# Re-ordering the issue lists of a fused SSM-convolution and token-MLP kernel, with the last spectrum pair's transfers on SyncE and GpSimd

## The chip, the cores and the metric

The kernel runs on one core of a Trainium2 chip. The metric is the device time of one execution in microseconds (us), taken as the median over runs. Besides the runs there is one profiled execution, from which every duration below is read. Times on the profile's axis count from the start of its span.

## The reference, cut to what matters

```python
def _A_ref(q, k, v, shift_k, ssm_k, ssm_D):        # S = 2048 tokens, D = 448 channels
    ...
    kv = k_shift * v                               # k filtered over 4 tokens, times v
    kv_f = rfft2(pad(kv, S)); kf_f = rfft2(pad(ssm_k, S))
    y = irfft2(kv_f * kf_f)[:S]                    # causal convolution of length 2048
    y = y + kv * ssm_D
    return q * y

def _B_ref(x, w1, b1, w2, b2):                     # F = 1792
    h = layernorm(x)
    u = gelu(einsum("bsd,sf->bdf", h, w1) + b1)    # the MLP mixes tokens, not channels
    y = einsum("bdf,fs->bds", u, w2) + b2
    return transpose(y)

x = A_q
h = x + _A_ref(layernorm(x), A_k, A_v, A_shift_k, A_ssm_k, A_ssm_D)
out = h + _B_ref(layernorm(h), B_w1, B_b1, B_w2, B_b2)
```

## The kernel before, in words

A token index is split in two: 128 partitions times 16 rows r. The convolution is done as a two-step Fourier transform on TensorE. Stage 1 (steps k1 and u1, L1060) transforms over one factor; its output is moved between partitions by SBUF-to-SBUF DMAs (L1076); stage 2 (k2 and u2, L1095) transforms over the other. Then the spectra of the filter and of kv are multiplied and transformed back. The way back is where the change lies.

**Inverse stage 1 (emit_products_i1).** It works on eight pairs jj of frequency groups. For each pair VectorE multiplies the two spectra (two products, L1161), TensorE does 16 matmuls (L1178), and ScalarE copies the two PSUM halves, h = 0 and 1, into the buffer TU (L739 in the profile, which is the helper that records every such copy). DMAs then carry the result from TU to the buffer TZ, where the partitions are those that the next stage contracts over. For seven of the pairs each of the two groups of a pair takes two DMAs (L1201): one of 196 KB for rows 0 to 13, by GpSimd (for one group of pair 1 by SyncE), and one of 28 KB for rows 14 and 15, by SyncE. The last pair, number 7, is cut differently, by halves h and groups par: four DMAs of 98 KB (L1190).

**Rows 0 and 1 in advance (emit_ct, NZ = 2).** The places of the last pair in TZ are filled with zeros for rows 0 and 1 (L1119), and what the last pair gives to these rows is added by extra matmuls (L1308) that read TU directly and use a small table EW. EW is filled by four DMAs of 4 KB from the table ET (L1128); these are the small table transfers.

**Inverse stage 2 (emit_i2).** For each row r two matmuls (L1300) contract TZ with the table ET. VectorE, ScalarE and GpSimd then apply the gate with the normalised input, take a layer norm (two rows at a time from row 2 on, with the powers on GpSimd at L1379) and write the normalised row Q (L1386 on VectorE). The PSUM copy is on VectorE for rows 0 to 3 (L1337), and else on ScalarE (L1317) or VectorE (L1319), as the order says; L1327 is VectorE's gate product and L1355 ScalarE's sum of squares.

**MLP (emit_mlp).** As soon as Q of row r is there, seven matmuls (L1433) add row r to the first seven chunks of the hidden layer; they hold seven of the eight PSUM banks, so that the rows of stage 2 that still come share one bank, each waiting for the copy of the one before it. Then come the other seven chunks (L1443), the GELUs, the second layer (L1455), the residual add (L1458) and the output DMAs. The weights of the first layer come in quarters w1a.0 to w1a.3 (L1406) and w1b (L1410), those of the second in w2 (L1417), all on SyncE's queue. w1a.1 waits for all four DMAs of the last pair.

**The order.** Every engine's instruction list is written out by hand, in the table ORDER at the top of the file, and each engine runs its list strictly in order; a scheduler only puts in the semaphore waits and picks the PSUM banks. A token such as i1.16:19 is step i1.16, operation 19. These tokens are used below:

| Token | What it is |
|---|---|
| i1.1, i1.4, i1.6, i1.8, i1.10, i1.12, i1.14, i1.16 | inverse stage 1 of pairs 0 to 7, in this order; on PE and ACT matmuls and copies, from 18 or 19 on the DMAs |
| i1.4:20 | the 196 KB DMA of pair 1 that SyncE issues; i1.4:18 is GpSimd's |
| i1.16:19, :20, :21, :22 | the last pair's DMAs: (h 0, par 0), (h 0, par 1), (h 1, par 0), (h 1, par 1) |
| i1.16:18, i1.16:9 | ScalarE's copies of the last pair's halves h 1 and h 0 |
| ct0.1:2 to :5 | the four small table transfers into EW (L1128) |
| i2.1, i2.9, i2.17, i2.20, i2.28, i2.32, i2.41, i2.45, i2.54, ... i2.84, i2.93, i2.97 | stage 2 matmuls of rows 0, 1, 2, 3, 4, 5, 6, 7, 8, ... 13, 14, 15; i2.2 and i2.10 are the extra matmuls of rows 0 and 1 |
| i2.3, i2.4, i2.5, i2.6, i2.7, i2.8 | row 0 behind its matmuls: gate, statistics on DVE, power on POOL (i2.7), Q on DVE (i2.8) |
| mlp.0 ... mlp.15 | the L1433 matmuls of row r, seven each |
| q.4 ... q.8, xn.* | statistics of the input rows (DVE L1237, L1239; powers POOL L1245, L1248) and the normalised input rows 0 to 3 (ACT L1270) |
| warm.* | 14 matmuls whose result is never read (L1211), put where TensorE would wait |

SyncE's list from the last pairs on, before:

```
i1.6:22 ct0.1:5 ct0.1:2-4 i1.4:20 i1.16:22 i1.16:20 i1.16:19 i1.1:20 i1.1:22 w1a.1:0
i1.12:22 i1.14:20 i1.4:21 i1.4:19 w1a.2:0 i1.6:20 i1.14:22 i1.10:20 i1.10:22 w1a.3:0
i1.8:22 i1.12:20 i1.8:20 w1b.0:0-3 w2.0:0-3
```

Of the kernel before, what the change touches and what calls it, by code (L numbers as in the profile page):

```python
# [36 lines left out]
        "mlp.15:1 mlp.15:5-6 mlp.15:3 mlp.15:2 mlp.17:0-15 mlp.18:0-15 mlp.19:0-15 mlp.20:0-15 mlp.21:0-15 "
        "mlp.22:0-15 mlp.23:0-15 mlp.24:0-13 mlp.25:0-13 mlp.26:0-13 mlp.27:0-13 mlp.28:0-13 mlp.29:0-13 "
# [545 lines left out]
def _build(nc, A_q, A_k, A_v, A_shift_k, A_ssm_k, A_ssm_D, B_w1, B_b1, B_w2, B_b2, out):  # L584
# [54 lines left out]
    with ctx:  # L639
        sch = _Sched(nc, ctx, n_dma_sems=112, small_off=SMALL)  # L640
        op = sch.op
# [509 lines left out]
        def emit_products_i1():  # L1151
            for jj in range(R // 2):
# [44 lines left out]
                for par in range(2):  # L1197
                    j = 2 * jj + par
# [319 lines left out]
```

## Time and profile before

| | |
|---|---|
| median of 3 runs | 173.64 us (172.6, 173.64, 174.01) |
| the profiled execution's own time | 173.4 us |
| its span | 171.6 us, so 1.8 us lie around the span |
| granted TensorE clock | 0.999 |
| busy over the span | PE 162.0 us, VectorE 101.4, ScalarE 92.6, GpSimd 59.5 |
| inverse stage 1, last pair's matmuls | 69.62 to about 71.3 us |
| stage 2 with the first MLP rows | 74.87 to 94.66 us |
| rest of the MLP | to about 169 us |

The page of the profile gives busy time by engine and the costliest groups. The view of the chain of waits goes back from the last instruction and says, in order of time, which engine or transfer held the end. The timeline gives start and duration of the instructions of one engine, merged where they follow each other, and in brackets the idle time before them and what ended it. Two things are needed to read TensorE here: a 448-column matmul has a duration of 0.35 us, but the next one starts 0.19 us later, so a wait costs what its start is late against the 0.19 us pitch, which is about 0.16 us more than the idle time in the bracket. And a wait for several semaphores is put down to the one that came last by the profile, which need not be the one that was waited for.

### The profile page before, as it was taken

The page shows a single profiled execution, that of the slowest core. Times are in us where ns is not written, and L with a number is a line of the kernel's source. Part 1 is how long each engine was busy: PE and PEld are TensorE (multiplying, and loading weights), DVE is VectorE, ACT ScalarE, POOL GpSimd, SP SyncE. Part 2 cuts the span into 40 slices and gives each one's busy share as a digit, 9 for nine tenths or more (in the row PEclk, how much of TensorE's full clock was granted, in tenths as well). Part 3 has the DMA queues.
Part 4 walks back from the last instruction along what each step waited for, and adds up shares of the span by engine and source line. Part 5 has one row for each costly group of instructions (what it writes and reads, how often), then busy time and mean ns, then how long its engine had stood idle before and what let it go on. Part 6 is the DMA issues. An engine that isn't in the chain of part 4 may idle for free.

```text
span 171.6 us, 3572 instructions
## 1 busy us (share of the span) xinstructions
PE 162.0 (94%) x1425; PEld 94.4 (55%) x1425; DVE 101.4 (59%) x188; ACT 92.6 (54%) x132; POOL 59.5 (35%) x151
## 2 busy tenths in 40 slices
PE   6979999889889999988999999999999999999994
PEld 2765745442334344543454555555567777777783
DVE  7998988859899999999979730000003133132231
ACT  3798688988999999989857526321210000000000
POOL 8347527590810586246887830000000000000000
PEclk9999999999999999999999999999999999999999
DMA  5999677685859756546999999991000111101111
GB/s 164 419 310 381 200 240 281 223 315 174 268 140 370 279 168 195 176 161 179 285 316 372 408 423 415 418 419 60 0 0 4 53 53 53 53 0 57 53 53 54
DMA packets 15652, 35.15 MB, mean 205 GB/s; under 512 B 3692, under 2 KB 9804, under 8 KB 15636
## 3 DMA queue, kind: packets, MB, share of 16 engines
q1 hardware_dynamic: 12588, 28.45, 46.0%
q0 software_dynamic: 2784, 6.29, 11.6%
q8 instruction: 11, 0.18, 0.4%
q10 hardware_dynamic: 264, 0.18, 0.3%
q14 instruction: 5, 0.04, 0.1%
HBM read 22.05 MB, written 1.84 MB: 139 GB/s over the span
## 4 chain that ended last, share of the span: by engine, by line
PE 64%; ACT 15%; DMA 9%; DVE 5%; SPq 2%; POOL 2%; issue 2%; DVEq 0%; POOLq 0%
PE ps L1455 25%; PE ps L1443 12%; PE ps L1433 9%; ACT arena L739 8%; PE ps L1095 5%; DMA arena<-in_A_ssm_k_dram 5%; ACT arena L1070 4%; DMA arena<-arena 4%; PE ps L1178 4%; PE ps L1060 3%; PE ps L993 2%; PE ps L1300 2%; DVE arena L1008 2%; ACT arena L740 2%; SPq L888 1%
## 5 line engine op out<-in xcount | busy, mean ns | idle before, releaser
L1458 DVE SCALAR_TENSOR_TENSOR arena<-ps,arena 128x448 bf16<-128x448 f32 (+2 forms) x17 | 11.1, 656 | 57.2 <-PE ps L1455 57.2
L1455 PE MATMUL ps<-arena 128*128 128x448 bf16 (+2 forms) x238 | 42.7, 342 | 0.0
L1455 PEld LDWEIGHTS ps<-arena 128*128 128x128 bf16 x238 | 33.3, 145 | 9.5
L739 ACT CAST arena<-ps 128x896 bf16<-128x896 f32 x30 | 24.6, 1013 | 0.2 <-PE ps L1095 0.2
L1433 PE MATMUL ps<-arena 128*128 128x448 bf16 x112 | 22.6, 353 | 0.2 <-DVE arena L1375 0.2
L1070 ACT CAST arena<-ps 128x896 bf16<-128x896 f32 x24 | 20.5, 915 | 3.8 <-PE ps L1060 3.7
L1076 POOL DMA_DIRECT2D arena<-arena x32 | 17.6, 556 | 13.1 <-ACT arena L1070 11.4
L1443 PE MATMUL ps<-arena 128*128 128x448 bf16 x112 | 21.4, 352 | 0.0
L1423 ACT ACTIVATE arena<-ps,arena 128x448 bf16<-128x448 f32 x14 | 8.3, 635 | 19.1 <-PE ps L1443 14.6
L1095 PE MATMUL ps<-arena 128*64 128x448 bf16 x128 | 15.2, 359 | 2.4 <-ACT arena L739 0.8
L1161 DVE TENSOR_TENSOR arena<-arena 128x1792 bf16<-128x1792 bf16 x16 | 16.7, 1085 | 0.3 <-ACT arena L739 0.2
L1433 PEld LDWEIGHTS ps<-arena 128*128 128x128 bf16 x112 | 10.8, 98 | 10.9 <-DVE arena L1386 1.2
L1443 PEld LDWEIGHTS ps<-arena 128*128 128x128 bf16 x112 | 11.0, 98 | 10.2
L1060 PE MATMUL ps<-arena 128*32 128x448 bf16 x256 | 15.0, 355 | 0.8 <-DVE arena L1008 0.5
L1178 PE MATMUL ps<-arena 64*128 64x448 bf16 x128 | 14.5, 351 | 0.1
L1201 POOL DMA_DIRECT2D arena<-arena x13 | 7.7, 599 | 13.7 <-ACT arena L739 13.7
L1095 PEld LDWEIGHTS ps<-arena 128*64 128x64 f16 x128 | 5.8, 108 | 10.8 <-ACT arena L739 2.9
L1178 PEld LDWEIGHTS ps<-arena 64*128 64x128 f16 x128 | 6.1, 94 | 8.2 <-ACT arena L739 2.5
L1008 DVE TENSOR_TENSOR arena<-ps,arena 128x512 bf16<-128x512 f32 (+1 forms) x16 | 9.1, 618 | 2.1 <-PE ps L993 1.8
L1355 ACT ACTIVATE arena<-arena 128x448 bf16<-128x448 f32 x14 | 8.0, 572 | 3.6 <-DVE arena L1327 3.5
L739 ACT COPY arena<-ps 128x1024 bf16<-128x1024 bf16 (+1 forms) x8 | 7.8, 1016 | 3.7 <-PE ps L967 2.9
L1386 DVE TENSOR_SCALAR arena<-arena 128x448 bf16<-128x448 f32 x16 | 7.7, 505 | 2.8 <-POOL arena L1379 2.8
(96 smaller groups left out, 192.1 us busy)
## 6 DMA issues: line engine op xcount, KB each, us to landing
arena<-in_B_w_dram SPq DMA_DIRECT2D x8, 896.0 KB, 7.2
arena<-in_B_w_dram SPq DMA_DIRECT2D x2, 2048.0 KB, 17.8
arena<-arena POOLq DMA_DIRECT2D x32, 112.0 KB, 3.3
arena<-arena SPq DMA_DIRECT2D x16, 224.0 KB, 3.1
arena<-in_B_w_dram SPq DMA_DIRECT2D x2, 1536.0 KB, 20.1
arena<-arena POOLq DMA_DIRECT2D x13, 196.0 KB, 4.2
arena<-in_A_k_dram SPq DMA_DIRECT2D x4, 448.0 KB, 5.8
arena<-in_A_v_dram SPq DMA_DIRECT2D x4, 448.0 KB, 9.1
```

Of the source, the lines that this page charges most:

```text
L739: return e.copy(out=dst(), in_=src())
L1008: return e.tensor_tensor(out=v, in0=u.rearrange("p t (r d) -> p t r d", d=64), in1=v, op=ALU.mult)
L1060: op("pe", lambda e, W, b=b, r=r, q=q, x=x, c0=c0: e.matmul(PS[32 * q:32 * q + 32, b.slots[x], 0:D], E[:, 2 * r + x, c0:c0 + 32], src[:, r ...
L1070: return e.copy(out=dst, in_=Ppair(b)) if W == "act" else e.tensor_copy(out=dst, in_=Ppair(b))
L1076: shuf[tag].append(op(q_, lambda e, W, g=g, i=i, a=a, nu=nu, jh=jh: e.dma_start(T[a + i:a + i + 4 * nu - 3:4].rearrange("p (j k) c d -> p ...
L1095: op("pe", lambda e, W, b=bs[h], h=h, j=j, c=c, par=par: e.matmul(PS[64 * par:64 * par + 64, b.slots[c], 0:D], FW[:, 64 * c:64 * c + 64], ...
L1161: op("dve", lambda e, W, m=m, i=i: e.tensor_tensor(out=MR(m.slots[0]).rearrange("p (x y) d -> p x y d", x=2), in0=TU[:, i].unsqueeze(2).br ...
L1178: k = op("pe", lambda e, W, b=bs[h], m=ms[h], par=par, t=t, tab=tab, xy=xy, P=P: e.matmul(Pb(b, par), tab[P, :], MR(m.slots[0])[P, xy, :], ...
L1433: op("pe", lambda e, W, r=r, fc=fc, b=bs[fc]: e.matmul(Pb(b), W1A[:, r, 128 * fc:128 * fc + 128], Q[:, r, :], start=(r == 0), stop=(r == R ...
L1443: op("pe", lambda e, W, r=r, fc=fc, b=b: e.matmul(Pb(b), W1B[:, r, 128 * (fc - n0):128 * (fc - n0) + 128], Q[:, r, :], start=(r == 0), sto ...
L1455: op("pe", lambda e, W, r=r, fc=fc, b=b, d0=d0, d1=d1: e.matmul(Pb(b)[:, d0:d1], W2[fc // 7][:, fc % 7, r:S:R], G[:, fc, d0:d1], start=(fc ...
L1458: op("dve", lambda e, W, r=r, b=b, A=A, d0=d0, d1=d1: e.scalar_tensor_tensor(out=X[:, r, d0:d1], in0=Pb(b)[:, d0:d1], scalar=bm[:, r:r + 1 ...
```

## The change

One line of code and the order lists. In emit_products_i1 the last pair's DMAs go to SyncE where h equals par (i1.16:19 and :22) and to GpSimd where it does not (:20 and :21); before, ScalarE issued :21 and SyncE the other three. In SyncE's list the small table transfers stand behind i1.10:20 instead of i1.6:22, and all 28 KB DMAs stand ahead of w1a.3. On TensorE, from the last pair on, the table transposes come first, the warm matmuls are spread (nine instead of eight behind the last pair's matmuls), and rows 2, 7, 3, 4, 6, 8, 5 are taken in this order instead of 4, 2, 7, 3, 6, 5, 8; row 11 comes behind mlp.3 instead of mlp.2, row 12 behind mlp.4 instead of mlp.3. On ScalarE and VectorE the order of the same operations changes, and rows 12 and 13 swap engines for their PSUM copy (i2.81 to VectorE, i2.85 to ScalarE). Up to the last pair's matmuls the lists of TensorE, ScalarE, VectorE and GpSimd are unchanged but for one warm matmul.

```diff
     "pe": (
...
-        "i1.4:16 warm.9:0 warm.11:0 warm.5:0 warm.8:0 warm.1:0 i1.16:1-7 i1.16:10-16 i1.16:8 i1.16:17 warm.10:0 "
-        "warm.4:0 warm.7:0 warm.6:0 warm.0:0 ct.2:0-7 warm.12:0 warm.3:0 ct.0:0-7 ct.1:0-6 warm.2:0 i2.1:0-1 "
-        "i2.2:0-3 i2.9:0 ct.1:7 i2.9:1 i2.10:0-3 i2.28:0-1 i2.17:0-1 i2.45:0-1 i2.20:0-1 i2.41:0-1 i2.32:0-1 "
-        "i2.54:0-1 mlp.0:6 mlp.0:1 mlp.0:5 mlp.0:2-4 mlp.0:0 i2.58:0-1 mlp.1:6 mlp.1:0 mlp.1:4 mlp.1:3 mlp.1:2 "
...
+        "i1.4:16 warm.9:0 warm.11:0 warm.5:0 warm.8:0 i1.16:1-7 i1.16:10-17 i1.16:8 ct.1:0-7 ct.0:0-7 ct.2:0-7 "
+        "warm.1:0 warm.10:0 warm.6:0 warm.3:0 i2.1:0-1 i2.2:0-3 i2.9:0-1 i2.10:0-3 warm.0:0 warm.2:0 i2.17:0-1 "
+        "i2.45:0-1 i2.20:0-1 warm.4:0 warm.7:0 i2.28:0-1 i2.41:0-1 warm.12:0 i2.54:0-1 i2.32:0-1 mlp.0:4 mlp.0:1 "
+        "mlp.0:5 mlp.0:3 mlp.0:6 i2.58:0-1 mlp.0:0 mlp.0:2 mlp.1:3 mlp.1:1 mlp.1:5 mlp.1:0 mlp.1:2 mlp.1:6 mlp.1:4 "
...
     "act": (
...
-        "xn.2:0 i1.16:18 i1.16:9 i1.16:21 ct.2:8 ct.0:8 xn.4:0 ct.1:8 xn.5:0 i2.29:0 i2.46:0 i2.19:0 i2.33:0 "
-        "i2.22:0 i2.42:0 i2.31:0 i2.59:0 i2.35:0 i2.68:0 i2.44:0 i2.48:0 i2.72:0 i2.57:0 i2.81:0 i2.61:0 i2.70:0 "
-        "i2.74:0 i2.94:0 i2.83:0 i2.87:0 i2.96:0 i2.100:0 mlp.16:0 mlp.16:4 mlp.16:2 mlp.16:1 mlp.16:5 mlp.16:3 "
+        "xn.2:0 i1.16:18 i1.16:9 ct.0:8 ct.1:8 ct.2:8 xn.4:0 xn.5:0 i2.46:0 i2.19:0 i2.22:0 i2.29:0 i2.42:0 i2.33:0 "
+        "i2.59:0 i2.31:0 i2.35:0 i2.44:0 i2.68:0 i2.48:0 i2.72:0 i2.57:0 i2.61:0 i2.70:0 i2.85:0 i2.74:0 i2.94:0 "
+        "i2.83:0 i2.87:0 i2.96:0 i2.100:0 mlp.16:1 mlp.16:5 mlp.16:0 mlp.16:6 mlp.16:4 mlp.16:2-3 mlp.17:16 "
...
     "dve": (
...
-        "q.4:0 q.4:2-3 q.4:1 q.3:1-3 q.5:0 q.5:2-3 q.5:1 q.6:2 q.6:0-1 q.7:0 q.7:2 xn.3:1 i2.3:0 q.6:3 i2.4:0 "
-        "i2.11:0 i2.5:0 i2.12:0 i2.6:0 i2.18:0 i2.21:0 q.7:3 i2.13:0 i2.8:0 i2.14:0 i2.55:0 i2.30:0 i2.16:0 q.7:1 "
-        "i2.34:0 i2.43:0 i2.26:0 i2.27:0 i2.47:0 q.8:0 q.8:2-3 q.8:1 i2.39:0 i2.56:0 i2.60:0 i2.40:0 i2.69:0 "
-        "i2.52:0 i2.53:0 i2.85:0 i2.73:0 i2.65:0 i2.66:0 i2.82:0 i2.86:0 i2.98:0 i2.78:0 i2.99:0 i2.95:0 i2.79:0 "
...
+        "q.3:2 q.3:1 q.3:3 q.4:2 q.4:0 q.4:3 q.4:1 q.5:2 q.5:0 q.5:3 q.5:1 q.6:2 q.6:0 q.7:0 q.7:2 q.6:3 q.6:1 "
+        "i2.3:0 xn.3:1 i2.4:0 i2.11:0 i2.5:0 i2.18:0 i2.6:0 i2.21:0 i2.12:0 q.7:3 i2.13:0 i2.8:0 i2.14:0 i2.55:0 "
+        "i2.30:0 i2.16:0 i2.34:0 i2.43:0 i2.26:0 i2.27:0 i2.47:0 q.8:0 q.8:2 q.8:1 q.8:3 i2.39:0 q.7:1 i2.56:0 "
+        "i2.60:0 i2.40:0 i2.69:0 i2.81:0 i2.52:0 i2.53:0 i2.82:0 i2.73:0 i2.65:0 i2.66:0 i2.95:0 i2.86:0 i2.79:0 "
...
     "pool": (
...
-        "i1.10:21 i1.1:19 i1.1:21 xn.0:0 i1.12:19 i1.12:21 i1.6:19 i1.6:21 i1.4:18 q.4:4-5 q.2:4-5 xn.3:0 q.6:4-5 "
-        "i2.7:0 i2.23:0-1 i2.15:0 i2.23:2 i2.24:0 i2.25:0 i2.36:0-2 i2.37:0 i2.49:0 i2.38:0 i2.49:1-2 q.8:4 i2.50:0 "
-        "q.8:5 i2.51:0 i2.62:0-2 i2.63:0 i2.64:0 i2.75:0-2 i2.76:0 i2.77:0 i2.88:0-2 i2.89:0 i2.90:0 i2.101:0-2 "
-        "i2.102:0 i2.103:0 i2.0:0 "
+        "i1.10:21 i1.1:19 i1.1:21 xn.0:0 i1.12:19 i1.12:21 i1.6:19 i1.6:21 i1.4:18 q.2:4-5 i1.16:21 i1.16:20 xn.3:0 "
+        "q.4:4-5 q.6:4-5 i2.7:0 i2.23:0-2 i2.15:0 i2.24:0 i2.25:0 i2.36:0-2 i2.37:0 i2.49:0 i2.38:0 i2.49:1-2 "
+        "i2.50:0 q.8:4-5 i2.51:0 i2.62:0-2 i2.63:0 i2.64:0 i2.75:0-2 i2.0:0 i2.76:0 i2.77:0 i2.88:0-2 i2.89:0 "
+        "i2.90:0 i2.101:0-2 i2.102:0 i2.103:0 "
     "sp": (
...
-        "ct0.1:1 ct0.1:0 w1a.0:0 xload.3:0 xload.1:0 i1.6:22 ct0.1:5 ct0.1:2-4 i1.4:20 i1.16:22 i1.16:20 i1.16:19 "
-        "i1.1:20 i1.1:22 w1a.1:0 i1.12:22 i1.14:20 i1.4:21 i1.4:19 w1a.2:0 i1.6:20 i1.14:22 i1.10:20 i1.10:22 "
-        "w1a.3:0 i1.8:22 i1.12:20 i1.8:20 w1b.0:0-3 w2.0:0-3 mlp.25:15 mlp.27:15 mlp.29:15 mlp.31:15 mlp.33:15 "
+        "ct0.1:1 ct0.1:0 w1a.0:0 xload.3:0 xload.1:0 i1.10:20 ct0.1:5 ct0.1:2-4 i1.6:22 i1.1:20 i1.1:22 i1.4:20 "
+        "i1.16:22 i1.16:19 w1a.1:0 i1.14:22 i1.14:20 w1a.2:0 i1.8:20 i1.8:22 i1.4:19 i1.4:21 i1.12:20 i1.12:22 "
+        "i1.10:22 i1.6:20 w1a.3:0 w1b.0:0-3 w2.0:0-3 mlp.25:15 mlp.27:15 mlp.29:15 mlp.31:15 mlp.33:15 mlp.35:15 "
...
-                            k = op("act" if h and par == 0 else "sp", lambda e, W, j=j, h=h, p0=p0: e.dma_start(
+                            k = op("sp" if h == par else "pool", lambda e, W, j=j, h=h, p0=p0: e.dma_start(
```

## The prediction

> **What bounds the kernel now.** I read the page's busy times first, then the chain of waits in order of time, then the windows, and last the timelines of TensorE (PE) and SyncE (SP).
>
> ```profile
> PE 162.0 (94%) x1425; PEld 94.4 (55%) x1425; DVE 101.4 (59%) x188; ACT 92.6 (54%) x132; POOL 59.5 (35%) x151
> ```
>
> PE is busy nearly throughout, so only its waits can be won, and the chain says where they are (start, length, what):
>
> ```profile
> 47.72 9.81 ACT arena L739 x12
> ...
> 71.72 1.62 ACT arena L739 x2
> ...
> 73.36 0.67 SPq L1190
> ...
> 74.07 3.66 DMA arena<-arena
> ...
> 77.78 1.70 PE ps L1300 x8
> ...
> 79.50 0.69 DVE arena L1337 x2
> ...
> 80.36 0.40 DVE arena L1386
> ...
> 80.83 1.56 PE ps L1433 x7
> ```
>
> ScalarE's copies carry the end up to 73.34, then the last pair's DMAs, then VectorE (DVE) up to the first MLP row. The windows (busy time of each engine) show who has room there:
>
> ```profile
> core 0: us, PE busy (x) PEld busy (x) DVE busy (x) ACT busy (x) POOL busy (x), PEclk, DMA share, GB/s
> ...
> 70.00:80.00 10.00, 8.97 (x70) 4.99 (x67) 9.59 (x28) 9.14 (x13) 4.84 (x9) 1.00 0.48 140
> 80.00:85.00 5.00, 4.79 (x26) 2.14 (x24) 5.00 (x18) 4.49 (x12) 4.05 (x10) 1.00 0.94 315
> ```
>
> DVE is as full as PE. PE's waits are four, of which these are the timeline's rows:
>
> ```profile
> 74.87 0.55 PE L1300 MATMUL ps<-arena 128*128 128x448 bf16 x2 [0.61 <-DMA arena<-arena]
> ...
> 77.78 2.82 PE L1300 MATMUL ps<-arena 128*128 128x448 bf16 x14 [0.41 <-DMA arena<-arena]
> 80.81 1.57 PE L1433 MATMUL ps<-arena 128*128 128x448 bf16 x7 [0.21 <-DVE arena L1375]
> ...
> 92.39 0.54 PE L1300 MATMUL ps<-arena 128*128 128x448 bf16 x2 [0.28 <-DVE arena L1327]
> ```
>
> Against the 0.19 us pitch they cost 0.77, 0.58, 0.37 and 0.44 us, 2.16 in all. After 94.66 PE runs without a wait, so the end moves by what the first row-8 matmul moves. SP's issues:
>
> ```profile
> 68.08 2.99 SPq L1128 DMA_DIRECT2D arena<-arena  x4
> 71.12 0.70 SPq L1201 DMA_DIRECT2D arena<-arena  x1
> 72.55 2.19 SPq L1190 DMA_DIRECT2D arena<-arena  x3
> 72.55 1.53 ACTq L1190 DMA_DIRECT2D arena<-arena  x1
> ...
> 84.36 0.43 SPq L1406 DMA_DIRECT2D arena<-in_B_w_dram  x1
> 84.82 2.10 SPq L1201 DMA_DIRECT2D arena<-arena  x3
> ```
>
> The last line answers the wait at 92.39. The bracket names VectorE, but its gate i2.85 that row 14 needs ended at 91.76; by the semaphores' updates these three 28 KB DMAs landed at 91.92, 92.11 and 92.30, and PE's sequencer stands on them one after another. They had queued behind w1a.3 (issued 84.36, landed 91.61).
>
> **The change part by part.** Up to 70.09 nothing that carries the end is moved: ScalarE's copies follow each other at their 0.80 pitch from 63.76 to 71, DVE is busy 10.00 of 10 us from 60 to 70, and both lists stand. I cost that at nothing.
>
> *Small table transfers.* The four L1128 issues (2.99 us) go from 68.08 to about 62.3, behind i1.10:20, whose copies end at 61.57. Nobody reads EW before 75.26, and it was complete at 72.85, so this alone gains nothing. But SP then reaches i1.4:20 when its copy ends (70.48) instead of 71.12, although i1.1:20 and :22 (0.70 each) now go ahead of it, as they fit into 68.0 to 69.4. i1.4:20 landed at 74.82 and released row 0 at 74.87. Its bounds: 0.6 earlier, if it again takes 3.7 us; or 74.82 as before, if it is GpSimd's own 196 KB transfers (landing up to 73.85) that hold it. I take 74.3, nearer to the first, as its packets ran back to back only from about 73.1.
>
> *The last pair.* SP issues :22 at 72.55 as before and :19 at 73.36 instead of 74.07, since :20 no longer stands ahead; with the 3.66 us of the chain it lands at 77.0. GpSimd (POOL) issues :21 and :20 0.29 us behind their copies (the delay of i1.4:18: 70.48 to 70.77), at 72.8 and 73.6, 0.59 us each. POOL's transfers took 2.9, 4.2 and 5.7 us at least, in the median and at most (L1201, 196 KB), the least of L1076 (112 KB) 2.2; so :20 lands between 75.8 and 79.3. I take the 3.1 us of i1.4:18, the last and the nearest in load: 76.7. So the last landing is 77.0 instead of 77.73. PE meanwhile has rows 0 and 1 and two warm matmuls, 2.8 us from 74.3, and reaches row 2 at 77.1.
>
> On POOL the two issues (1.2 us) and their waits push the power of q.4 from 72.4 to 73.8 to about 74.5 to 75.9; it is wanted by ScalarE's gate of row 7 at about 78, and POOL's next, q.6, waits for DVE until 76 anyway. ScalarE loses an issue of 1.53 us, of which 0.80 was idle time ahead of the table copies (74.13); these come 0.8 earlier, but row 4 waited for the DMAs and not for them. xn.4 now waits for an operation that DVE does behind i2.3, so 76.7 instead of 76.02; its reader i2.18 runs at 78.0.
>
> One rule of the Trainium skill speaks against giving DMAs to POOL: "SBUF — State Buffer", section "SBUF: two separate sides", says that GpSimd cannot write its descriptors while VectorE runs an operation in a two-port mode (copies and the like). It gives 620 ns growing to 3100 ns; with that 2.5 us on top (an estimate from that page) :20 would land at 79.2 and the time would be that of the late-transfer rival below. The rows between 72.23 and 75.40 on DVE are only L1237 and L1239, batch-norm statistics, which the page does not list; I give it little weight.
>
> *VectorE.* From 70.09 to the end of i2.8 (80.75) both lists hold the same 29 operations in another order. Its idle time there is 0.23 us ahead of i2.3 and some hundredths. So however early the data come, Q of row 0 is there no earlier than about 80.45. By the new order: i2.3 at 76.0, i2.18 at 78.0 if row 2's matmuls start by 77.3, and i2.8 ends at 80.5; mlp.0 starts at 80.6 instead of 80.81. PE reaches it at 77.1 + 3.23 (seven rows and three warm matmuls) = 80.3. The first two waits of PE thus mostly turn into waits for DVE: **0.2 us gained** of the 1.72.
>
> *Row 14.* w1a.1 is issued once the last pair has landed (77.05 instead of 77.75), then two small DMAs, w1a.2 at about 78.9, eight small ones of 0.70 to 84.6, and w1a.3. w1a.2 took 7.0 us, so lands at 85.9, and the small ones 0.2 us after each other behind it (as they did at 88.24 to 88.87): 87.5 at the latest, 4 us ahead of row 14. w1a.3 is issued at 84.6 instead of 84.36 and wanted by mlp.12 at over 99: hidden by 8 us. **0.44 us gained.**
>
> *New waits.* Row 12's PSUM copy on DVE needs POOL's q.8 power (end 89.52), and behind it in DVE's list stand i2.52 and i2.53, for which mlp.6 and mlp.7 wait. i2.52 itself waited for POOL until 90.19, and 89.55 + 0.67 = 90.22, so this costs nothing unless that power slips. Row 13's copy goes to ScalarE, ahead of a square; row 14's waits for the square of row 11 there, about 0.1. Row 5's copy ends at 82.2 and mlp.0's last matmul needs its bank, about 0.1. Bounds: nothing, or two full waits such as the 0.37 and 0.44 above, 0.8. **I take 0.2 lost**, as each handoff but these two has room.
>
> Sum: -0.2 - 0.44 + 0.2 = -0.44, say -0.4. The profiled execution took 173.4 (span 171.6 and 1.8 around it), 0.24 below the median of the runs, 173.64. 173.4 - 0.4 = **173.0 us**.
>
> **The rivals.**
>
> *Nothing left.* The new waits cost 0.6 to 0.8 and eat the gain: 173.4 to 173.6. For it: one PSUM bank passes from row to row, and DVE is 5.00 of 5 busy from 80 to 85. Against: PE stood there only for the two reasons named.
>
> *Slower: POOL's transfer lands late.* Rows 2 on need all four DMAs, and DVE's list has i2.6, and so row 0's Q, behind i2.18 of row 2. Landing up to 77.3 costs nothing; beyond it, mlp.0 comes 3.4 us behind the landing. With the slowest row, 5.7 us from 73.6, that is 79.3 and mlp.0 at 82.7, 1.9 later; with row 14's 0.44 won and 0.2 lost, 173.4 + 1.9 - 0.24 = 175.1. It turns slower than before when :20 takes over 4.0 us (0.24 us more than mlp.0's start of before). For it: 6 of the 13 L1201 transfers on POOL took over 4.2 us. Against: all six were issued between 59 and 68.2 with others of POOL's in flight; of the 13, the first and the last, which met least, took 3.0 and 3.1, and by 73.9 POOL's have all landed.
>
> *Faster: PE is the bound.* All four waits go, less the one warm matmul that moved behind the last pair (0.19): 2.16 - 0.19 = 1.97, 171.4 us. Against it stands DVE's count above.
>
> **How the numbers follow.** Likeliest (-0.4, own range 172.6 to 173.4) 0.63; nothing left 0.18; late transfer 0.14; faster 0.05. A difference of 1%, 1.7 us, is about what a measurement of this kernel can tell from no change. The late case's 175.1 lies just at that bound, so half of its chance is put beyond; the faster case lies beyond as a whole. So faster 0.05, same 0.88, slower 0.07. The range leaves out the faster case and the upper part of the late one, and takes in that single runs of before spread by 0.6 to each side: 172.1 to 174.6.
>
> **What would show it.** L1300 should start near 74.3 and, with row 2, near 77.1; the bracket at 80.6 should name DVE (L1375 or L1386) and be larger than 0.21; the two POOL issues of L1190 should stand at 72.8 and 73.6; the bracket of row 14 should be gone and the 28 KB DMAs landed by 88. I am wrong if row 2 starts after 77.7, if mlp.0 starts before 80.3 (then DVE was not the bound), or if PE waits anew by more than 0.5 us between 81 and 95.

## The result, and the profile after

The changed kernel took 175.19 us in the median (173.31 to 177.93, 22 runs), the kernel before, measured beside it, 173.55 (172.34 to 175.71, 22 runs). The ratio is 1.0055, with a 95% interval of 1.0029 to 1.0081: slower, though by less than the 1% named in the prediction; 173.0 was forecast, and 174.6 was the upper end. In 11 of the changed kernel's 22 runs the mean granted TensorE clock was 0.99 or less (175.32 us and above); the other eleven have a median of 174.20, which is 0.65 above before. For before's runs of this comparison no clock is on record. To read the numbers here and in the table below: a ratio leaves the longest runs out, a median does not.

The profiled execution took 174.95 us (span 173.0) at clock 1.0, against 173.4 (171.6). So it shows the loss without the clock. Line numbers are one higher than before; in the experiments they differ by one either way. From the page, its busy times:

```profile
PE 161.7 (93%) x1425; PEld 94.7 (55%) x1425; DVE 101.0 (58%) x188; ACT 92.6 (53%) x132; POOL 61.0 (35%) x153
...
```

PE has the same work to 0.3 us, in a span that is 1.4 us longer. From the chain of waits, in order of time (start, length, what):

```profile
70.16 1.13 ACT arena L740
72.51 0.72 POOL arena L1249
73.62 2.84 DMA arena<-arena
77.02 0.77 PE ps L1309 x4
77.81 0.68 DVE arena L1338
80.47 0.68 DVE arena L1338 x2
...
93.93 0.73 POOL arena L1380
95.69 0.63 POOL arena L1287
96.97 0.74 POOL arena L1380
97.73 0.95 DVE arena L1387 x2
98.72 8.12 PE ps L1434 x42
```

Two places are new. A DMA ends just ahead of row 0, not of row 2 as before (the chain starts it at GpSimd's issue of 73.62, but row 0 reads nothing of the last pair; by the semaphores' updates it stood for i1.4:20, landed at 76.39, and i1.4:18, landed at 76.01). And at 95.69 a GpSimd operation, L1287, has come onto the chain. The timeline of PE has the two waits:

```profile
73.82 0.54 PE L1212 MATMUL ps<-arena 128*128 128x448 f16 x2
76.48 0.54 PE L1301 MATMUL ps<-arena 128*128 128x448 bf16 x2 [2.12 <-DMA arena<-arena]
...
79.12 1.30 PE L1301 MATMUL ps<-arena 128*128 128x448 bf16 x6
...
82.36 1.12 PE L1434 MATMUL ps<-arena 128*128 128x448 bf16 x5
...
93.43 0.54 PE L1301 MATMUL ps<-arena 128*128 128x448 bf16 x2
...
98.72 1.50 PE L1434 MATMUL ps<-arena 128*128 128x448 bf16 x7 [0.21 <-DVE arena L1387]
```

Four brackets before have become two. Against the 0.19 us pitch the one at 76.48 costs 2.28 us and the one at 98.72 costs 0.37, together 2.65 where before had 2.16. Row 2 (79.12), the first MLP row (82.36) and row 14 (93.43) start without one. VectorE stood idle too while row 0 was late:

```profile
76.25 0.23 DVE L1240 BATCH_NORM_AGGREGATE arena<-arena 128x2 f32<-128x6 f32 x2
77.81 0.68 DVE L1338 SCALAR_TENSOR_TENSOR arena<-ps,arena 128x448 f32<-128x448 f32 x1 [1.33 <-PE ps L1309]
```

The queues of SyncE and then GpSimd, where the two issues of the last pair stand as they were meant to:

```profile
63.22 3.28 SPq L1129 DMA_DIRECT2D arena<-arena  x4
68.07 3.92 SPq L1202 DMA_DIRECT2D arena<-arena  x4
73.35 1.48 SPq L1191 DMA_DIRECT2D arena<-arena  x2
```

```profile
73.62 0.66 POOL L1191 DMA_DIRECT2D arena<-arena  x1 [0.39 <-ACT arena L740]
74.44 0.60 POOL L1191 DMA_DIRECT2D arena<-arena  x1 [0.15 <-issue]
...
95.64 0.66 POOL L1287 TENSOR_TENSOR arena<-arena 128x16 f32<-128x16 f32 x1
```

**How times are compared below.** The whole axis is shifted: ScalarE's last copy of pair 1, which releases that pair's transfers, ends at 71.28 instead of 70.48. That 0.80 us is not the change's. It is already there at a copy ahead of inverse stage 1's matmuls (it ends at 50.23 against 49.42), and between these two copies lie 21.06 us in both; over the profiles of this study, of either list, that point moved by 2 us where the clock was full. So stages are counted from the end of that copy, here called T:

| from T, us | before | after |
|---|---|---|
| i1.4:20 issued, landed | 0.64, 4.34 | 0.03, 5.10 |
| row 0 starts | 4.39 | 5.19 |
| mlp.0 starts | 10.33 | 11.08 |
| row 14 starts | 21.92 | 22.14 |
| mlp.8 starts | 24.18 | 24.41 |
| mlp.17 (second half of the hidden layer) starts | 34.78 | 35.39 |

Row 0 comes 0.80 later and mlp.0 0.75; 0.53 of this is won back between mlp.0 and row 14, and 0.38 is lost behind mlp.8: 0.61 in the stage, which with the 0.80 of the shift and 0.14 around and behind makes the 1.55 us between the two profiled executions.

### The profile page after: what moved, and what is told of

Same layout as the page of the kernel before. It is cut to its first block, busy times and chain, and to the rows that moved or that the text cites. A ratio compares the mean times of both kernels' runs of the same rounds, so it can differ in the third digit from the quotient of the medians.

```text
span 173.0 us, 3574 instructions
## 1 busy us (share of the span) xinstructions
PE 161.7 (93%) x1425; PEld 94.7 (55%) x1425; DVE 101.0 (58%) x188; ACT 92.6 (53%) x132; POOL 61.0 (35%) x153
## 4 chain that ended last, share of the span: by engine, by line
PE 57%; ACT 13%; DMA 11%; POOL 7%; DVE 6%; issue 2%; SPq 2%; DVEq 0%; POOLq 0%
PE ps L1456 24%; PE ps L1444 12%; ACT arena L740 7%; DMA arena<-arena 6%; PE ps L1096 5%; DMA arena<-in_A_ssm_k_dram 5%; PE ps L1434 5%; ACT arena L1071 4%; PE ps L1179 4%; PE ps L1061 2%; POOL arena L1380 2%; ACT arena L741 2%; PE ps L994 1%; DVE arena L1387 1%; POOL arena L1376 1%
## 5 line engine op out<-in xcount | busy, mean ns | idle before, releaser
L1434 PE MATMUL ps<-arena 128*128 128x448 bf16 x112 | 22.8, 353 | 0.2 <-DVE arena L1387 0.2
L1444 PE MATMUL ps<-arena 128*128 128x448 bf16 x112 | 21.4, 352 | 0.0
L1301 PE MATMUL ps<-arena 128*128 128x448 bf16 x32 | 8.0, 352 | 2.1 <-DMA arena<-arena 2.1
```

What stands on the lines that cost most here:

```text
L1434: op("pe", lambda e, W, r=r, fc=fc, b=bs[fc]: e.matmul(Pb(b), W1A[:, r, 128 * fc:128 * fc + 128], Q[:, r, :], start=(r == 0), stop=(r == R ...
L1444: op("pe", lambda e, W, r=r, fc=fc, b=b: e.matmul(Pb(b), W1B[:, r, 128 * (fc - n0):128 * (fc - n0) + 128], Q[:, r, :], start=(r == 0), sto ...
```

## The experiments

Eighteen runs follow, each beside before on the same chip; e1 to e3, e6 to e9, e10 to e15 and e16 to e19 (in the order of the table) share a chip each, so a comparison across these groups is also one across chips. "Clock" counts the runs with a mean granted clock below 0.995, of this kernel and of before there. The columns on the right are from each one's profile, in us from T (landed: the later of i1.4:20 and i1.4:18); "wait" is PE's wait ahead of row 0 over the pitch.

| kernel | ratio, 95% | median | clock, before's | landed | wait | mlp.0 | mlp.17 |
|---|---|---|---|---|---|---|---|
| before | | | | 4.34 | 0.77 | 10.33 | 34.78 |
| after | 1.0055 [1.0029, 1.0081] | 175.19 | 11/22, not on record | 5.10 | 2.28 | 11.08 | 35.39 |
| e1_after_i11_behind | 1.0089 [1.0055, 1.0122] | 175.05 | 4/8, 0/31 | 4.81 | 1.99 | 10.78 | 35.10 |
| e4_before_head | 1.0047 [1.0014, 1.0079] | 174.16 | 2/12, 0/31 | 4.84 | 1.27 | 10.69 | 34.61 |
| e5_before_head_i11_behind | 1.0055 [1.0021, 1.0088] | 174.06 | 2/12, 0/31 | 4.71 | 1.18 | 10.60 | 34.51 |
| e3_before_small_ahead_w1a3 | 1.0010 [0.9987, 1.0034] | 173.32 | 0/12, 0/31 | 5.03 | 1.45 | 10.88 | 34.79 |
| e6_after_old_head | 1.0027 [0.9998, 1.0056] | 173.80 | 0/12, 1/35 | 4.80 | 1.93 | 10.75 | 35.06 |
| e7_before_head_hold | 1.0012 [0.9988, 1.0036] | 173.11 | 0/12, 1/35 | 4.97 | 1.40 | 10.83 | 34.73 |
| e8_before_i4_early | 1.0012 [0.9986, 1.0037] | 173.56 | 0/12, 1/35 | 4.86 | 1.34 | 10.75 | 34.66 |
| e9_after_hold | 1.0057 [1.0029, 1.0086] | 174.33 | 4/12, 1/35 | 5.48 | 2.61 | 13.11 | 37.42 |
| e10_before_one_small_pool | 0.9965 [0.9918, 1.0012] | 173.64 | 2/12, 5/35 | 4.63 | 1.11 | 10.52 | 34.52 |
| e11_after_warm_fill | 1.0031 [0.9981, 1.0081] | 175.63 | 5/12, 5/35 | 5.79 | 2.03 | 11.69 | 35.97 |
| e13_old_head_row10 | 0.9964 [0.9923, 1.0006] | 173.49 | 3/12, 5/35 | 4.72 | 1.85 | 10.66 | 34.60 |
| e15_before_fewer_warm | 0.9966 [0.9916, 1.0017] | 174.03 | 7/12, 5/35 | 4.39 | 2.33 | 11.87 | 35.78 |
| e16_after_again | 1.0100 [1.0060, 1.0139] | 175.88 | 4/9, 2/32 | 5.76 | 2.93 | 13.42 | 37.73 |
| e17_after_full_fill | 1.0063 [1.0032, 1.0094] | 174.44 | 0/12, 2/32 | 4.96 | none | 11.17 | 35.45 |
| e18_old_head_row10_fill | 1.0050 [1.0021, 1.0079] | 173.93 | 1/12, 2/32 | 4.66 | none | 11.17 | 35.06 |
| e19_pair1_by_sp | 0.9995 [0.9964, 1.0026] | 173.11 | 0/12, 2/32 | 4.38 | 0.81 | 10.24 | 34.24 |
| e20_after_repaired | 1.0047 [0.9998, 1.0096] | 173.75 | 1/12, 4/17 | 5.32 | 1.51 | 11.18 | 35.08 |
| e21_repaired_i11_behind | 1.0008 [0.9981, 1.0035] | 173.47 | 3/12, 3/17 | 4.87 | 1.06 | 10.73 | 34.63 |

**First: the head of SyncE's list.** The theory was that i1.1:20 and :22, now issued just ahead of i1.4:20, delay it; the rivals that its own early issue beside GpSimd's i1.4:18 does, or that the loss lies in the rest of the change.

```diff
# e1: after, SyncE
-  i1.6:22 i1.1:20 i1.1:22 i1.4:20 i1.16:22 i1.16:19
+  i1.6:22 i1.4:20 i1.16:22 i1.16:19 i1.1:20 i1.1:22
# e4: before, SyncE
-  i1.6:22 ct0.1:5 ct0.1:2-4 i1.4:20 i1.16:22 i1.16:20 i1.16:19 i1.1:20 i1.1:22
+  i1.10:20 ct0.1:5 ct0.1:2-4 i1.6:22 i1.1:20 i1.1:22 i1.4:20 i1.16:22 i1.16:20 i1.16:19
# e5: before, SyncE
-  i1.6:22 ct0.1:5 ct0.1:2-4 i1.4:20
+  i1.10:20 ct0.1:5 ct0.1:2-4 i1.6:22 i1.4:20
# e3: before, SyncE
-  w1a.3:0 i1.8:22 i1.12:20 i1.8:20
+  i1.8:22 i1.12:20 i1.8:20 w1a.3:0
```

> The changed kernel with the two 28 KB transfers i1.1:20 and i1.1:22 put back behind the last pair's two on SyncE's list. The number to read is when i1.4:20 lands behind the end of ScalarE's last copy of pair 1: 4.34 us in the kernel before, 5.11 us in the changed one. Queue theory (the two small transfers ahead of i1.4:20 on the same eight DMA engines hold it): 4.3 us or less, row 0 starts 0.8 to 1.1 us earlier, and the time is 0.6 to 1.0 us below the changed kernel's, so level with the kernel before or up to 0.4 us below it. Sharing theory (SyncE reaches i1.4:20 earlier, so it shares the engines with GpSimd's i1.4:18 and both end late, whatever is ahead): 5.0 us again, and the time of the changed kernel.

> The kernel before with only the head of SyncE's list from the change: i1.10:20 and the four table transfers first, then i1.6:22, i1.1:20, i1.1:22, i1.4:20. Queue theory and sharing theory both: i1.4:20 lands 5.0 to 5.2 us behind pair 1's last copy, row 0 starts 0.7 us later than in the kernel before, the time is 0.4 to 0.8 us above it. If the cause of the loss lies elsewhere (the last pair on GpSimd, or the orders of the other engines): 4.0 to 4.3 us and the time of the kernel before.

> The kernel before with the table transfers early (i1.10:20 and the four L1128 transfers ahead of i1.6:22), but i1.1:20 and i1.1:22 left behind the last pair. Queue theory: i1.4:20 lands 3.7 to 4.3 us behind pair 1's last copy, time equal to the kernel before within 0.3 us or below. Sharing theory: 5.0 us, time 0.4 to 0.8 us above the kernel before.

> The kernel before with only the last three 28 KB transfers moved ahead of w1a.3 on SyncE's list. The prediction's step on row 14: the three land by 90 instead of 91.9 to 92.3, the wait of 0.28 us ahead of row 14's matmuls (0.44 against the pitch) goes, and the time is 0.3 to 0.45 us below the kernel before. Rival: row 14 then waits for the copy of row 13 on VectorE or ScalarE instead, and nothing is gained beyond 0.1 us.

The head of the list alone makes before slower by 0.5% (e4, e5), and taking the two i1.1 transfers out of the way mends neither this (e5) nor the changed kernel (e1, no shorter in the median). The landings of e1 and e5, 4.81 and 4.71, lie between what the two theories expected. In e4 and e5 i1.4:20 is issued 0.03 us behind the copy instead of 0.64, and the later of the pair's two still lands at 4.84 and 4.71. Where the 0.5% goes, their profiles do not show: mlp.17 starts at 34.61 and 34.51, no later than before's 34.78. And e3, where i1.4:20 was issued late, at 1.14, landed at 5.03; with the same head as before, e10 and e15 below landed at 4.63 and 4.39. So the 4.34 in before's profile was the best of four cases. e3 also bears on row 14's wait: the 28 KB transfers had landed at 18.13 instead of 21.83, the wait was gone, and the time was the same.

**Second: is the early issue itself the harm?** e7 and e9 hold i1.4:20 back by an added wait for ScalarE's xn.1, so that it is issued about as late as before; e8 only issues i1.4:20 early, ahead of two of the four tables, and e6 puts the old head into the changed kernel.

```diff
# e6: after, SyncE
-  i1.10:20 ct0.1:5 ct0.1:2-4 i1.6:22 i1.1:20 i1.1:22 i1.4:20 i1.16:22 i1.16:19
+  i1.6:22 ct0.1:5 ct0.1:2-4 i1.4:20 i1.16:22 i1.16:19 i1.1:20 i1.1:22
# e7: e5, and e9: after; added ahead of the emission
+            hold["i1.4:20"].preds.append(hold["xn.1:0"].id)
# e8: before, SyncE
-  ct0.1:5 ct0.1:2-4 i1.4:20
+  ct0.1:5 ct0.1:2 i1.4:20 ct0.1:3-4
```

> The changed kernel with the head of SyncE's list as it was before: i1.6:22, the four table transfers, i1.4:20, the last pair's two, then i1.1:20 and :22; i1.10:20 goes to the tail. Everything else is the change's (last pair on GpSimd, the orders of the other engines, the 28 KB transfers ahead of w1a.3). If the head is the cause: i1.4:20 lands at most 4.4 us behind pair 1's last copy, row 0 starts 0.7 us earlier than in the changed kernel, and the time is 0.7 to 1.0 us below it, level with the kernel before. If the other orders or GpSimd's transfers are the cause: the time stays 0.7 us or more above the kernel before.

> The kernel before with the table transfers early, as in the run before this with i1.1:20 and :22 left behind, but i1.4:20 also waits for the end of ScalarE's xn.1, which puts its issue back to 0.64 us behind pair 1's last copy, where it was in the kernel before. Sharing theory (the early issue of i1.4:20 beside GpSimd's i1.4:18 costs): i1.4:18 lands about 3.4 us and i1.4:20 4.3 us behind the copy, and the time is that of the kernel before within 0.3 us. If the early table transfers themselves cost, by holding up GpSimd's transfers: 0.6 to 0.9 us above it again.

> The kernel before with only i1.4:20 earlier: two of the four table transfers are issued behind it instead of ahead of it, so it is issued 0.03 us behind pair 1's last copy and the table transfers stay where they were in time. Sharing theory: i1.4:20 and i1.4:18 land together, 4.5 to 5.1 us behind the copy, and the time is 0.5 to 0.9 us above the kernel before. If the early table transfers cost: the time of the kernel before or a little less, i1.4:20 landing 3.7 us behind the copy.

> The changed kernel with i1.4:20 also waiting for the end of xn.1, so that it is issued 0.6 us later. Sharing theory: it lands earlier by being issued later, 4.3 to 4.6 us behind the copy instead of 5.1, and the time is 0.5 to 0.8 us below the changed kernel's. If the order in SyncE's queue or the early table transfers cost: it lands 5.1 us or more behind the copy, and the time is the changed kernel's or more.

Issued at 0.66 (e7), 0.03 (e8), 0.79 (e6) or 0.65 (e9), pair 1 landed at 4.97, 4.86, 4.80 and 5.48: the landing does not follow the issue. The times leave the question open: e7 has 1.0012 where e5, the same but for the hold, had 1.0055 on another chip, as the sharing theory expected; but e8, which issues early, has 1.0012 too, and e9, held back, is no better than after. e6 takes about half of the loss away and had no low clock (0 of 12); e9 keeps both. The packets of the two queues in the traces suggest why an early issue gains nothing: before, SyncE's 1792-byte packets for i1.4:20 ran only from 2.5 us behind T, when GpSimd's transfers in flight were nearly through, at some 75 ns each; in after SyncE's queue (i1.1's two, then i1.4:20) had packets moving from T on, at 74 to 119 ns each (means of half a microsecond) between GpSimd's, and i1.4:18 itself then landed at 4.73 instead of 3.37. The Trainium skill, "DMA: Bandwidth & Descriptors", section "Issuing engines are not separate DMA queues", says that transfers of all issuing engines run on the same DMA engines and interleave; the trace agrees.

**Third: four steps by themselves.**

```diff
# e10: before, e3's edit, and i1.6:20 from SyncE to GpSimd, just ahead of i1.4:18
# e11: after, PE
-  warm.3:0 i2.1:0-1
+  warm.3:0 warm.0:0 warm.2:0 warm.4:0 warm.7:0 warm.12:0 i2.1:0-1
# e13: e6; GpSimd, then VectorE
-  i2.75:0-2 i2.0:0 i2.76:0 ... i2.103:0
+  i2.75:0-2 i2.76:0 ... i2.103:0 i2.0:0
-  i2.79:0 i2.78:0
+  i2.78:0 i2.79:0
# e15: before, six warm matmuls instead of fourteen, none behind the last pair
```

> Edit: before, with the last three 28 KB transfers ahead of w1a.3 (as in the small-ahead run) and one 28 KB transfer of pair 1's group, i1.6:20, taken from SyncE and issued by GpSimd just ahead of its i1.4:18. Theory A (i1.4:20 and i1.4:18 wait on one another because both lie on the same half of the 16 DMA engines, and GpSimd's transfers alternate between halves): i1.4:18 now goes to the other half, i1.4:20 lands 3.5 to 3.8 us behind ScalarE's copy instead of 4.3 to 5.0, row 0 starts about 1 us earlier, mlp.0 is then set by VectorE at about 10.1 behind that copy (typical 10.8), and the time is 0.3 to 0.7 us below before. Theory B (the landing is set by all the bytes in flight together, whichever engines carry them): i1.4:20 lands 4.3 to 5.0 behind the copy, row 0 at 4.4 to 5.1, and the time equals before's within 0.3%.

> Edit: after, with the five filler matmuls that stood between the rows of the last stage (warm.0, 2, 4, 7, 12) moved ahead of row 0; work and number of instructions are the same. Theory A (half of after's runs are long because PE stands idle for 2.3 us and more ahead of row 0, and the granted clock then halves for a few us): the wait falls from 2.28 to about 1.3 us, runs with a mean granted clock of 0.99 or less become rare (0 to 2 of 10, against 11 of 22), and the median falls by 0.6 to 1.2 us to about 174.0. Theory B (the lower clock has another cause in after, such as the DMA load at the time): four to six of ten runs stay at 0.99 or less, and the median stays at 174.5 to 175.2.

> Edit: the run of after with the old head of SyncE's list, and besides GpSimd's i2.0 put last again and, on VectorE, row 10's i2.78 ahead of row 11's i2.79. Theory A (the wait of 0.37 us ahead of mlp.10 comes from GpSimd's 0.67 us for i2.0 ahead of row 10's products): that wait goes, the stretch from row 0 to mlp.17 shortens by 0.3 to 0.45 us, and the ratio is 0.2 to 0.25% below the 1.0027 of that run, at 0.999 to 1.002. Theory B (the wait only moves to the next MLP row, since VectorE or PSUM banks bound it anyway): another wait of 0.2 to 0.4 us stands between mlp.8 and mlp.12 and the ratio stays at 1.002 to 1.004.

> Edit: before without eight of its fourteen filler matmuls (six are left); what is left out is only matmuls whose result nobody reads. Theory A (a long wait of PE ahead of row 0 halves the granted clock): the wait ahead of row 0 grows from 0.8 to 1.4 us to 2.3 to 2.9 us, a third or more of the runs show a mean granted clock of 0.99 or less (before: 1 in 66), and the median rises by 0.8 to 2 us though less work is done. Theory B (idle time of PE does not touch the clock; after's long runs come from elsewhere): the clock stays at 1.0 and the time is that of before within 0.3%, as row 0 is released by the same transfer.

e10's theory fell: i1.4:20 landed at 4.24 and i1.4:18 at 4.63. e13 confirms the second wait, though not which of its two edits removed it: behind mlp.9 PE runs through without one (before mlp.10 stood a bracket of 0.21), and from mlp.8 to mlp.17 it takes 10.59 us, where after took 10.98. Its timeline:

```profile
96.77 0.54 PE L1299 MATMUL ps<-arena 128*128 128x448 bf16 x2
97.15 10.76 PE L1432 MATMUL ps<-arena 128*128 128x448 bf16 x56
```

e15 makes before wait 2.33 us ahead of row 0 by taking fillers away, and the clock drops behind it, though less work is done: 7 of its 12 runs were low, 5 of 35 of before's there. Its median rose by only 0.32 us, not by the 0.8 to 2 expected; without low clocks it would have fallen, as the median of the runs above 0.995 is 172.65 against before's 173.40. In its timeline the pitch of the L1307 matmuls rises to 0.37 us (1.54 us for four) instead of 0.19 (0.92); its windows show the granted clock at 0.66:

```profile
75.79 0.55 PE L1299 MATMUL ps<-arena 128*128 128x448 bf16 x2 [2.17 <-DMA arena<-arena]
76.18 1.54 PE L1307 MATMUL ps<-arena 128*128 128x448 bf16 x4
```

```profile
75.00:80.00 5.00, 4.21 (x14) 1.88 (x15) 3.18 (x9) 4.33 (x5) 2.15 (x4) 0.66 0.44 109
80.00:85.00 5.00, 4.39 (x24) 2.02 (x23) 4.99 (x18) 4.41 (x10) 2.59 (x7) 1.00 0.89 298
```

e11 was inconclusive (5 of 12 low). On this chip before itself had low clocks in 5 of 35 runs, and e11's profile shows another place for them, at 10 to 20 us, where PE waits for the input loads and nothing is changed:

```profile
10.00:20.00 10.00, 8.90 (x118) 5.61 (x117) 6.72 (x13) 7.77 (x9) 4.06 (x8) 0.83 0.80 281
75.00:80.00 5.00, 3.13 (x25) 1.70 (x23) 3.47 (x10) 3.88 (x5) 4.20 (x8) 1.00 0.52 157
```

**Fourth: the clock again, on one chip, and pair 1 on one queue.** e16 is the changed kernel unedited.

```diff
# e17: after, PE; N_WZ 14 -> 21, seven more warm matmuls
-  warm.1:0 warm.10:0 warm.6:0 warm.3:0 i2.1:0-1
+  warm.1:0 warm.10:0 warm.6:0 warm.3:0 warm.0:0 warm.2:0 warm.4:0 warm.7:0 warm.12:0 warm.14:0 ... warm.20:0 i2.1:0-1
# e18: e13 with the same fill
# e19: e5; SyncE, and the engine of the 196 KB transfers
-  i1.6:22 i1.4:20
+  i1.6:22 i1.4:18 i1.4:20
-  "sp" if j == 3 else "pool"
+  "sp" if j in (2, 3) else "pool"
```

> Edit: none, the changed kernel as it is, for the share of its runs at a lower clock on the chip of this call. Theory A (the wait ahead of row 0 halves the granted clock for some us in about half of its runs): 3 to 8 of 12 runs at 0.99 or less while before has at most 1 in 10. Theory B (a matter of the chip of the first session): no more runs at 0.99 than before's share.

> Edit: the changed kernel with the nine fillers that stood near or behind row 0, and seven more of 0.19 us, put together ahead of row 0; nothing else. Theory A (the wait halves the clock): the wait of 2.28 us falls below 0.7, no run has its dip behind row 0, so runs at 0.99 or less fall to before's share, and the median falls by 0.5 to 1.2 us below that of the changed kernel on this chip, to 173.7 to 174.3. Theory B (the dips have another cause): the share stays at that of the changed kernel and the median with it.

> Edit: the old head of SyncE's list, i2.0 last on GpSimd, row 10's i2.78 ahead of row 11's i2.79 on VectorE, and the fill of the run before. Theory A: the three repairs add up; from row 0 to mlp.17 29.8 us as without the fill (34.60 less 4.77), no dips behind row 0, time 0 to 0.5 us below before (ratio 0.997 to 1.000). Theory B (row 0's landing decides alone): ratio 1.002 to 1.004 like the run with the old head.

> Edit: before, with SyncE's tables early, i1.1:20 and i1.1:22 behind the last pair and the last three 28 KB transfers ahead of w1a.3, as in the run so made, and GpSimd's i1.4:18 given to SyncE just ahead of i1.4:20. Theory A (GpSimd's descriptors and the interleaving with its packets hold pair 1 up; on one queue the two follow each other at 1.1 to 1.5 us): i1.4:18 lands at 3.0 to 3.4 behind ScalarE's copy, i1.4:20 at 4.0 to 4.4, row 0 starts 0.4 to 0.8 us earlier than in that run (4.80), and the time is 0.4 to 0.8 us below its ratio of 1.0055. Theory B (the bytes that GpSimd's earlier transfers still have to move over the same engines hold everything up): row 0 at 4.6 to 5.0 as there, time the same.

(The expectation of e19 says that the last three 28 KB transfers were moved ahead of w1a.3; as the diff shows, they were not.) The clock theory held. Of e16's runs 4 of 9 were low, of e17's none of 12, on a chip where before had 2 of 32, and the median fell by 1.44 us, from 175.88 to 174.44, though seven matmuls were added. Without the low runs the two medians are 174.50 and 174.44, so the difference lies in the low runs. e16's profile caught such a run; its timeline of PE and its windows:

```profile
76.72 0.54 PE L1301 MATMUL ps<-arena 128*128 128x448 bf16 x2 [2.77 <-DMA arena<-arena]
77.10 0.92 PE L1309 MATMUL ps<-arena 128*128 128x448 bf16 x4
77.85 0.91 PE L1301 MATMUL ps<-arena 128*128 128x448 bf16 x2
78.55 1.70 PE L1309 MATMUL ps<-arena 128*128 128x448 bf16 x4
80.05 0.95 PE L1212 MATMUL ps<-arena 128*128 128x448 f16 x2
```

```profile
75.00:80.00 5.00, 3.28 (x12) 1.47 (x13) 2.42 (x7) 2.64 (x4) 2.36 (x4) 0.79 0.40 98
80.00:85.00 5.00, 5.00 (x24) 2.31 (x23) 4.14 (x14) 3.21 (x8) 1.76 (x5) 0.87 0.98 336
```

Behind a wait of 2.93 us the matmuls go on at full pitch for 1.2 us, then from 77.9 to 81.3 at 0.37 us each; mlp.0 comes 7.58 us behind row 0 instead of 5.89, which is 1.7 us lost on top of the wait. In e17 the fillers run up to row 0, and the matmuls behind it keep the full pitch (four in 0.92 us):

```profile
73.79 2.62 PE L1211 MATMUL ps<-arena 128*128 128x448 f16 x13
76.43 0.54 PE L1300 MATMUL ps<-arena 128*128 128x448 bf16 x2
76.81 0.92 PE L1308 MATMUL ps<-arena 128*128 128x448 bf16 x4
...
77.94 0.92 PE L1308 MATMUL ps<-arena 128*128 128x448 bf16 x4
```

The rest of the loss stays: 174.44 against 173.15 for before on that chip. The fill was also longer than needed (row 0 at 5.36, its data at 4.96), and in e18 it cost more, 5.37 against 4.66; from row 0 to mlp.17 e18 took 29.70 us, as expected, but its ratio of 1.0050 does not show that the three repairs add up. e19 landed as expected: 18 at 3.41 and 20 at 4.38, row 0 starts at 4.43 instead of e5's 4.80, and the ratio falls from 1.0055 to 0.9995, with no low clock. Part of this need not be the one queue: the chip is another than e5's, and i1.4:20 is issued at 0.77 instead of 0.03, as late as in e7, which had 1.0012.

**Fifth: the changed kernel mended.**

```diff
# e20: after with e19's engine edit, i2.0 and i2.78 as in e13, fillers as in e11
-  i1.6:22 i1.1:20 i1.1:22 i1.4:20 i1.16:22 i1.16:19
+  i1.6:22 i1.1:20 i1.1:22 i1.4:18 i1.4:20 i1.16:22 i1.16:19
# e21: e20, SyncE
-  i1.6:22 i1.1:20 i1.1:22 i1.4:18 i1.4:20 i1.16:22 i1.16:19
+  i1.6:22 i1.4:18 i1.4:20 i1.16:22 i1.16:19 i1.1:20 i1.1:22
```

> Edit: the changed kernel with GpSimd's i1.4:18 given to SyncE just ahead of i1.4:20, i2.0 last on GpSimd with row 10's i2.78 ahead of row 11's i2.79 on VectorE, and the five fillers from between the rows put ahead of row 0. Theory A (these three are the loss): row 0 at 4.4 to 4.6 behind ScalarE's last copy of pair 1, mlp.17 at 34.2 to 34.6 (before 34.78, changed kernel 35.39), no wait at mlp.10, no more runs at clock 0.99 than before, ratio 0.996 to 1.001. Theory B (something else of the change costs as well, the early tables for one): ratio 1.003 to 1.006.

> Edit: the last run's kernel (the changed kernel with the three repairs) with i1.1:20 and i1.1:22 put behind the last pair's transfers on SyncE again. Theory A (these two, issued just ahead, delay pair 1 on the same queue and engines): i1.4:20 lands 4.3 to 4.6 behind the copy instead of 5.32, row 0 at 4.4 to 4.7, mlp.17 at 34.1 to 34.4 instead of 35.08, ratio 0.996 to 1.000. Theory B (the spread of the landing is chance): landing 4.7 to 5.4, mlp.17 at 34.5 to 35.1, ratio 1.001 to 1.005.

e20 lost the wait at mlp.10 and the extra low clocks, but pair 1 landed late, at 5.32. So one queue by itself did not bring the landing forward here. With the two i1.1 transfers moved behind (e21) it landed at 4.87 and mlp.17 started at 34.63, both as the theory of chance expected; the kernel is level with before (1.0008), but on another chip than e20, and their intervals overlap. So e21 by itself does not show that these two transfers count. Over all profiles it looks so: with them ahead in the changed kernel and its relatives the landing was 5.10, 5.48, 5.79, 5.76, 4.96 and 5.32; with them behind, or with the old head, 4.81, 4.80, 4.72, 4.66 and 4.87. Against it stands e4, 4.84 with them ahead in before's lists, and e1's time, no shorter than after's. No kernel here beat before by more than its interval; nearest are e10 and e13, 0.35% and 0.36% below with intervals that reach above 1.

## Why the prediction was wrong, point by point

**Upstream of the last pair: right.** From the copy ahead of inverse stage 1 to T it is 21.06 us in both.

**Small table transfers: the step that failed.** The bounds of i1.4:20's landing were 0.6 us earlier, or as before. The second was taken from one profile and treated as the worst case, though the prediction itself names GpSimd's transfers as what may hold it. From T the prediction allowed 3.7 to 4.34 and took 3.8; after's profile has 5.10, and in 19 other profiles the later of the pair's two transfers landed at 4.34 to 5.79. An issue 0.6 us earlier brought it ahead of 4.34 in none of them. Row 0 so started 0.80 us later than before (5.19 against 4.39), and 1.4 us later than forecast (3.8); row 2 started at 7.84, past the 7.2 (77.7 on before's axis) that the prediction had named as a sign of being wrong. From T the forecast had mlp.0 at 10.12 and mlp.17 at 34.34; they came at 11.08 and 35.39, so 0.96 of the 1.05 us missed in the stage were there at mlp.0. What made the landing late is only in part known: the packets point to GpSimd's transfers and to the two i1.1 transfers issued ahead, and no run here settles how much each does.

**The clock: put at nothing.** The prediction took the 2.16 us of waits as idle time and no more. In the changed kernel the table transposes and fillers are done by 74.4, so the later row 0 is, the longer the one wait ahead of it: 2.28 us in the profile, 2.93 in e16. The prediction counted the fillers between the rows as work to get through, and did not ask what it means that only four are left ahead of row 0 where before had eight. With the wait at that length about half of the runs were at the lower clock (11 of 22, 4 of 9), and the one profiled lost 1.7 us on top of the wait. By e16 against e17 this is worth 1.4 us in the median. The runs at full clock have a median of 174.20, inside the range that was forecast; it is the clock that takes the median of all runs past its end.

**The last pair: right.** GpSimd's issues stood 0.3 us behind their copies, and the transfers took 3.47 and 3.56 us (3.1 forecast); row 2 ran 2.64 us behind row 0 without a wait. The slower rival, GpSimd's transfer landing late, did not happen; that its 175.1 is near the measured 175.19 is chance. Nor did the effect cited from the Trainium skill, "SBUF — State Buffer": 3.47 and 3.56 us lie within the 2.9 to 5.7 of before. But from 71.65 to 76.48 VectorE ran only batch-norm statistics, so no two-port copy was there to test the rule.

**VectorE: right in its length, not binding.** mlp.0 was forecast 6.3 us behind row 0 at the forecast start, as VectorE would be full; with row 0 late VectorE stood idle for 1.33 us, and mlp.0 came 5.89 us behind row 0 (5.94 before). So 0.75 of the 0.80 us by which row 0 came later went through to mlp.0.

**Row 14: right that the wait goes, but the gain hangs on row 0.** It is gone in after, but also in e4, e5, e7 and e8, whose 28 KB transfers still land at 19 to 21.5 us from T: there row 0, and with it PE, comes later and no longer runs ahead of them. So PE's waits could not simply be added up: before, with row 0 at 4.39, and e3, with row 0 at 5.07, reach mlp.17 at 34.78 and 34.79. With row 0 early the gain is there: in e19 row 0 starts at 4.43, the last 28 KB transfer lands at 20.61 instead of 21.83, some 0.1 us is left of the wait, and mlp.17 starts at 34.24, though e19's runs are only level with before's.

**New waits: right in kind, one mis-sized.** Forecast 0.2 in all. Measured 0.37 at mlp.10, at a place that was not named: i2.0, put ahead of i2.76 on GpSimd, took 0.66 us, and VectorE did row 11's i2.79 ahead of row 10's i2.78 (with both put back, e13 has no wait there). The bound of 0.8 held.

What stays open: how the landing varies from run to run, since each profile is one sample (4.96 to 5.79 for nearly the same lists), and how much of after's remaining 1.3 us on e17's chip the two i1.1 transfers, i2.0 and the interleaving each account for. e21 shows only that mended together they leave 0.08%, with an interval of 0.27 either way.

## What to carry to other kernels

A landing time read from one profile is a sample: before a step is bounded by it, see whose packets move at the same time, and let the upper bound go beyond what that profile shows. Waits of one engine that follow each other are not independent: a later one can be the slack that an early start left, so their sum is a gain only if none of them grows. And when filler matmuls are moved, look at how long PE then stands still at the worst landing, not at the usual one.

## What the runs showed of the hardware

The granted clock fell by half behind waits of 2.2 to 2.8 us. In the profiles with PE idle ahead of row 0 for 2.17, 2.45 and 2.77 us (e15, e9, e16) the pitch of 448-column matmuls went from 0.19 to 0.37 us, beginning 0.5, 1.0 and 1.2 us after PE had started again and lasting 3.4 us in each; with 2.12 us in after, 1.86 in e11 and 1.77 in e6 it stayed at 0.19. The Trainium skill, "TensorE: Matmul & The Clock Gate", section "Why this matters for your kernels", advises no idle gaps above about 3 us, and its "What's actually happening" gives a free-running window of 3.4 us. The length of the slow stretch agrees with that window, and its late start with a window that runs freely. The limit does not: here 2.2 us was enough in e15.

The clock records of the traces give a reason why only some runs pay. Each slow stretch begins a whole number of 3.413 us after the first full-clock record: 71.68 us (21 times) in e9, e15 and e16, 6.83 and 10.24 us (twice and three times) in e11 and e13. On that grid PE's idle time inside the one window ahead of the slow stretch was 2.38, 2.17 and 2.24 us in e9, e15 and e16; in the other traces with clock records no window up to the end of the stage held more than 1.77 us (e6; in after the 2.12 us were split, 1.66 us in one). So where a wait falls on the grid may decide whether it costs the clock. No run was made to test this, and the early slow stretches of e11 and e13, in a stage of smaller matmuls, followed windows with only 1.1 and 1.0 us idle.
